# Attention and a feed-forward on one core: scores on quarters of the array, four sums on VectorE, q's turn ahead of the queue, a product between two steps

## The chip, the cores and the metric

The kernel runs on one core of a Trainium2 chip. The metric is the device time of one execution in microseconds (us). The kernel before took 1366.23 us (median of three runs, 1366.04 to 1366.33).

The core's engines have queues of their own and run beside each other. In this text PE is TensorE (matrix products, into the eight banks of PSUM), DVE is VectorE, ACT is ScalarE, POOL is GpSimd, and SP is SyncE, which here only issues DMAs. Each engine takes its instructions in the order in which the code issues them.

## The reference

The first part is attention with normalized q and k: batch 8, 12 heads, 448 tokens, head size 64.

```python
def rmsnorm(x, g):
    rms = np.sqrt(np.mean(x * x, axis=-1, keepdims=True) + 1e-06)
    return x / rms * g
q_n, k_n = (rmsnorm(q, g_q), rmsnorm(k, g_k))
scores = (1.0 / np.sqrt(64)) * np.matmul(q_n, k_n.transpose(0, 1, 3, 2))
attn = softmax(scores)
attn_out = np.matmul(attn, v)
```

Its output is laid out as `x` with 3584 tokens (8 x 448) and 768 columns (12 x 64). The second part is a feed-forward with 2048 inner columns:

```python
h = np.maximum(x @ w_in, 0.0)
return (h * h @ w_out).astype(np.float32)
```

`w_in` (768 x 2048) and `w_out` (2048 x 768) arrive as 64-bit floats; everything else is float32.

## The kernel before

**Pairs of heads.** Attention works on 48 pairs: pair `i` holds two heads (index `e`) of one batch, so that their 2 x 64 columns fill 128 partitions. Its q and k are turned into `qT` and `kT` of 128 x 448. Keys come in blocks `m` of 128: three whole ones (`NJ = 3`) and a rest of 64, and the rests of an even pair and the next odd one are worked on together (`m == NJ`). `score` multiplies block `m` of keys with all queries, for both heads, into two banks; ACT's exponential (`weigh`, line 468) reads them and takes k's norm as its scale. POOL adds the weights up (`add_up`, L487), `attend` (L552, L567, L588) multiplies them with v, and the sums over keys (L604, L622, L631) divide at the end.

`score` has two forms. Where `whole(i)` holds (pairs 25 and on), a block of keys is cut in halves of 64: four matmuls with 64 rows and 64 columns, each on a quarter of the array (L449). Elsewhere it is two matmuls with 64 rows and 128 columns (L460). The rests are always in quarters (L460). A float32 matmul is two instructions in the profile, and a weight load stands before each.

**Turning q and k.** Early pairs are turned by PE (`turn`, L415, and L418 for the rest) after POOL has scaled q (L219). Pairs from 14 on are turned by DVE in blocks (`turn_blocks`, L372), from a layout that DMAs have brought; for q, ACT then multiplies with the gains (L382). `turn_among` puts this into the queue `tasks`, whose entries (squares, row sums, divisions, turns) are issued one or two for each product of the feed-forward.

**Feed-forward in units.** Unit `u` takes the four half batches of batches `2u` and `2u + 1` with two halves of the columns as a 2 x 2 block matrix, and makes each product by seven half-size products instead of eight, with sums of blocks on both sides. The inner columns come in four blocks; each has a first product (into `hid`, followed by relu and square on ACT) and a second one with `w_out` (L1216 for the rows that are left over, L1274). Unit 0 runs beside the attention of pairs 13 to 24, units 1 and 2 beside the later ones, and the last unit, 3, alone. In units 1 to 3 the first product uses the seven-product form twice, one inside the other (`deep_products`, L1077).

**Weights.** Pieces of the weights are loaded, converted to float32 (ACT L1698 to L1701, DVE L1712 and L1731) and summed into the forms that the seven products need. These sums wait in `sums_to_make` and are issued by `make_sum` (L1807), one for each step of the stream; `sum_engines` hands them to DVE and POOL in turn. For a `w_out` tile they are T1, T3, T2, T4, in this order; T2 is made from T1 and T4 from T2. In the second product of unit 0, P5 uses T1, then P6 uses T2 and P4 uses T4. The four sums of the left side are POOL's (L1202). Two `w_out` tiles belong to a block; the first block's weights are ready during the first stage, the others' in the block before their use or in their own.

**The last unit.** Its first products run in 28 steps of 11 matmuls, cut into four parts each and interleaved: part 2 and 3 of a step stand between parts of the next. After part 2 and part 3, DVE and ACT add the banks into `whole_hid`; each block ends with joins on POOL and DVE (L1134). The second products are in two levels as well and run in rounds (`ROUNDS`, L1602): for each form of `w_out`, named `right`, the inner forms are its quarters and their sums. `sum_right` makes these (L744): for the first round (`n = 0`) its sums 0, 1 and 2 on POOL during the first products, and sum 3 on DVE at the start of the round. `multiply_rest` (L1510) makes the products of 128 rows that no round covers, in four calls: at the first round and at `right == "21"` the two parts of the left half, at `"22"` and behind the last round the two parts of the right half.

Of the kernel before, what the change touches and what calls it, by code (L numbers as in the profile page):

```python
# [23 lines left out]
P = 128  # L24
# [201 lines left out]
def program(ctx, tc, rows, v, g, wide, ones, moe_w_in, moe_w_out, out, shift):  # L226
# [216 lines left out]
    def score(i, m):  # L443

        scs = banks_of(i, m)
        if whole(i) and m < NJ:
            for e, sc in enumerate(scs):
                for half in range(2):
                    nc.tensor.matmul(  # L449
                        sc[ds(half * D, D)],  # L450
                        lhsT=turned[i, 1][ds(e * D, D), ds(m * P + half * D, D)],
                        rhs=turned[i, 0][ds(e * D, D), :], start=True, stop=True,
                    )
            return
# [922 lines left out]
    def last_unit():  # L1377
# [46 lines left out]
        def sum_right(n, m):  # L1424
            b11, b12, b21, b22 = [right_of(n, t, k) for t in range(2) for k in range(2)]
            t1, t2, t4 = [more_rights[n % 2][:, k] for k in range(3)]
            dst, left, right = ((t1, b12, b11), (t2, b22, t1), (t4, t2, b21), (b12, b22, b12))[m]
            less(nc.vector if m == 3 else nc.gpsimd, dst, left, right)()

        for n, cost in enumerate(  # L1430
# [3 lines left out]
            if n == 28:  # L1434
                load_right(0)
                load_rest("11")
            elif n in (60, 64, 68, 72):
                sum_right(0, (n - 60) // 4) if n < 72 else None
        ffn_p.release()
# [9 lines left out]
        bank_sets = [[banks[n] for n in (0, 2, 3)], list(roles)]  # L1449
        rest_banks = [banks[4], banks[1]]  # L1450

# [49 lines left out]

        def multiply_rest(a, half, n):
            ends = n == len(ROUNDS) - 1
            size = Q if ends else HALF
            for at in range(0, HALF, size):
                some = slice(at, at + size)
                for blk in range(NBLK):
                    for t in range(2):
                        last = blk == NBLK - 1 and t
                        nc.tensor.matmul(  # L1510
                            rest_banks[half][:, some], lhsT=flat[a][:, blk, t, ds(NT * P, P)],
                            rhs=rights[n % 2][:, 2 * blk + t, some],
                            start=blk + t == 0 and n in (0, 4),
                            stop=bool(last and n not in (0, 4)), skip_group_check=True,
                        )
                if n not in (0, 4):
                    to = rest_acc[:, half * HALF + at : half * HALF + at + size]
                    nc.scalar.copy(to, rest_banks[half][:, some])
                    nc.sync.dma_start(
                        out[ds(2 * u * S + P * NT, P), ds(half * HALF + at, size)], to  # L1520
                    )

        def store_pair(pair, acc, e, half):
# [37 lines left out]
        for n, (name, right) in enumerate(ROUNDS):  # L1561
            if right == "11":
                multiply_rest(0, 0, n)
            elif right == "21":
# [170 lines left out]
    def make_weight_forms(kind, dst, t):  # L1735
# [7 lines left out]
        (in_sb if kind == "in" else out_sb)[t] = dst  # L1743
        sums_to_make.extend(todo)
        if kind == "out":
# [55 lines left out]
    def make_sum():  # L1801
# [3 lines left out]
        if sums_to_make:  # L1805
            to, left, right, op = sums_to_make.popleft()
            next(sum_engines).tensor_tensor(out=to, in0=left, in1=right, op=op)  # L1807
        elif forms_to_store:
            later.append([3, partial(nc.sync.dma_start, *forms_to_store.popleft())])
# [309 lines left out]
    def turn_among(i, x):  # L2119
        if in_blocks(i):  # L2120
            tasks.append(lambda: turn_blocks(i, x))
        else:
# [84 lines left out]
```

## Time and profile before

| | before |
|---|---|
| median of three runs | 1366.23 us |
| the profiled execution | 1367.66 us |
| its span, first to last instruction | 1365.9 us |
| PE busy | 1337.1 us (98%) |
| DVE / ACT / POOL busy | 874.6 / 612.5 / 769.6 us |
| attention alone | 0 to 128 us |
| first unit beside attention | 128 to 476 us |
| last unit's first products | 1094 to 1210.5 us |
| last unit's rounds | 1210.5 to 1365.9 us |

The profile is of one execution. A row of the timeline gives the start and length in us, engine, line, operation, output and inputs, shape, and the number of instructions merged; in brackets the idle time of the engine before it and what ended that. For PE, `64*128` is rows times columns of the array in use. A row of groups gives, behind the count, the busy us and the mean ns of one, then the idle time before them.

### The profile page before, as it was taken

The page shows a single profiled execution, that of the slowest core. Times are in us where ns is not written, and L with a number is a line of the kernel's source. Part 1 is how long each engine was busy: PE and PEld are TensorE (multiplying, and loading weights), DVE is VectorE, ACT ScalarE, POOL GpSimd, SP SyncE. Part 2 cuts the span into 40 slices and gives each one's busy share as a digit, 9 for nine tenths or more (in the row PEclk, how much of TensorE's full clock was granted, in tenths as well). Part 3 has the DMA queues.
Part 4 walks back from the last instruction along what each step waited for, and adds up shares of the span by engine and source line. Part 5 has one row for each costly group of instructions (what it writes and reads, how often), then busy time and mean ns, then how long its engine had stood idle before and what let it go on. Part 6 is the DMA issues. An engine that isn't in the chain of part 4 may idle for free.

```text
span 1365.9 us, 20475 instructions
## 1 busy us (share of the span) xinstructions
PE 1337.1 (98%) x6672; PEld 887.9 (65%) x6672; DVE 874.6 (64%) x1728; ACT 612.5 (45%) x1135; POOL 769.6 (56%) x751
## 2 busy tenths in 40 slices
PE   7999999999999999999999999999999999999998
PEld 3333444444444477676858577675858599999997
DVE  4897555886768766555556866556555855456672
ACT  6985576757757144343434344343433134330000
POOL 5668754655565879577567879577555732110010
PEclk9999999999999999999999999999999999999999
DMA  5666846967849877584847767674736465544542
GB/s 136 164 182 158 211 104 158 273 186 190 270 117 284 256 193 224 142 224 107 253 104 214 216 174 226 162 216 123 237 82 227 143 194 192 155 138 150 156 161 90
DMA packets 416632, 245.61 MB, mean 180 GB/s; under 512 B 273284, under 2 KB 381060, under 8 KB 415492
## 3 DMA queue, kind: packets, MB, share of 16 engines
q1 hardware_dynamic: 416224, 244.15, 63.3%
q8 instruction: 55, 0.90, 0.3%
q14 instruction: 61, 0.50, 0.1%
q10 hardware_dynamic: 292, 0.07, 0.0%
HBM read 178.13 MB, written 65.99 MB: 179 GB/s over the span
## 4 chain that ended last, share of the span: by engine, by line
PE 82%; DVE 5%; DMA 3%; POOL 3%; ACT 2%; issue 2%; SPq 2%; POOLq 0%; ACTq 0%; DVEq 0%
PE bank L1077 25%; PE bank L1274 19%; PE bank L1602 9%; PE bank L1016 7%; PE bank L449 4%; PE bank L567 4%; PE bank L460 4%; PE bank L552 3%; PE bank L1510 2%; PE bank L588 1%; PE bank L604 1%; DVE acc L1638 1%; DMA in_sb<-in_deep 1%; PE bank L631 1%; PE bank L1216 1%
## 5 line engine op out<-in xcount | busy, mean ns | idle before, releaser
L1077 PE MATMUL bank<-xT,in_sb 128*128 128x224 f32 x1344 | 287.0, 353 | 0.0
L1077 PEld LDWEIGHTS bank<-xT,in_sb 128*128 128x128 f32 x1344 | 253.1, 190 | 9.4 <-ACT wT L468 5.6
L468 ACT ACTIVATE wT<-bank,rr 128x448 f32<-128x448 f32 x288 | 163.9, 631 | 159.4 <-PE bank L449 98.1
L1274 PE MATMUL bank<-out_sb,hid 128*128 128x384 f32 x576 | 205.9, 490 | 2.8 <-POOL out_sb L1807 1.4
L204 POOL TENSOR_TENSOR rr<-ms,minus_half 128x8 f32<-128x8 f32 (+1 forms) x96 | 145.7, 1517 | 69.2 <-DVE ms L197 58.9
L1638 DVE TENSOR_TENSOR acc<-acc,bank 128x384 f32<-128x384 f32 x231 | 122.1, 546 | 77.1 <-PE bank L1274 59.1
L1274 PEld LDWEIGHTS bank<-out_sb,hid 128*128 128x128 f32 x576 | 107.7, 190 | 82.3 <-issue 7.7
L1274 PE MATMUL bank<-out_sb,sums 128*128 128x384 f32 x432 | 156.0, 491 | 1.3 <-DVE acc L1638 0.9
L1016 PE MATMUL bank<-xT,in_sb 128*128 128x448 f32 x336 | 131.8, 546 | 0.0
L1274 PEld LDWEIGHTS bank<-out_sb,sums 128*128 128x128 f32 x432 | 80.3, 190 | 67.2 <-issue 4.8
L487 POOL TENSOR_TENSOR sum<-sum,wT 128x448 f32<-128x448 f32 (+1 forms) x96 | 112.9, 1197 | 7.5 <-ACT wT L468 6.0
L1016 PEld LDWEIGHTS bank<-xT,in_sb 128*128 128x128 f32 x336 | 62.1, 190 | 68.8 <-issue 61.7
L460 PE MATMUL bank<-qT,kT 64*128 64x448 f32 (+1 forms) x492 | 102.7, 571 | 3.4 <-ACT qT L382 2.3
L1060 DVE TENSOR_TENSOR hid<-hid,bank 128x224 f32<-128x224 f32 x208 | 73.4, 382 | 43.9 <-PE bank L1077 40.8
L487 POOL TENSOR_TENSOR sum<-wT 128x448 f32<-128x448 f32 x48 | 55.8, 1184 | 66.4 <-ACT wT L468 66.4
L449 PE MATMUL bank<-qT,kT 64*64 64x448 f32 x552 | 76.1, 540 | 0.7 <-ACT wT L468 0.7
L460 PEld LDWEIGHTS bank<-qT,kT 64*128 64x128 f32 (+1 forms) x492 | 35.4, 166 | 63.5 <-issue 35.8
L1077 PE MATMUL bank<-more,in_sb 128*128 128x224 f32 x288 | 74.4, 353 | 0.8 <-DVE whole_hid L1060 0.8
L567 PE MATMUL bank<-wT,vt 64*64 64x448 f32 x576 | 73.9, 545 | 0.0
L382 ACT ACTIVATE qT<-qT,g 128x448 f32<-128x448 f32 x34 | 22.7, 666 | 111.1 <-DVE qT L372 111.1
L1701 ACT ACTIVATE words<-words 128x384 f16<-128x384 f32 x64 | 68.5, 1071 | 2.0
L1549 POOL TENSOR_TENSOR acc<-acc 128x768 f32<-128x768 f32 x2 | 4.3, 2136 | 106.3 <-DVE acc L1500 99.4
(200 smaller groups left out, 2401.9 us busy)
## 6 DMA issues: line engine op xcount, KB each, us to landing
in_sb<-in_deep SPq DMA_DIRECT2D x64, 384.0 KB, 3.8
in_sb<-in_deep SPq DMA_DIRECT2D x80, 256.0 KB, 4.4
out_sb<-out_forms SPq DMA_DIRECT2D x48, 384.0 KB, 5.6
words<-in_moe_w_in_dram SPq DMA_DIRECT2D x32, 384.0 KB, 3.7
words<-in_moe_w_out_dram SPq DMA_DIRECT2D x32, 384.0 KB, 3.6
out_forms<-out_sb SPq DMA_DIRECT2D x8, 1536.0 KB, 6.4
qk<-in_q_dram SPq DMA_DIRECT2D x96, 96.0 KB, 2.5
qk<-in_k_dram SPq DMA_DIRECT2D x96, 96.0 KB, 2.6
```

The lines of the kernel that those rows point to most:

```text
L204: self.nc.gpsimd.tensor_tensor(out=self.rr[i][:, x, 0 : self.count(i)], in0=ms, in1=self.minus_half.to_broadcast(list(ms.shape)), op=ALU.pow,)
L449: nc.tensor.matmul(sc[ds(half * D, D)], lhsT=turned[i, 1][ds(e * D, D), ds(m * P + half * D, D)], rhs=turned[i, 0][ds(e * D, D), :], start ...
L460: nc.tensor.matmul(sc[some], lhsT=turned[p, 1][r, keys], rhs=turned[p, 0][r, :], start=True, stop=True,)
L468: nc.scalar.activation(new_weights((i, m), e), sc, AF.Exp, scale=rows.rr[i][:, 1, 2 * m + e : 2 * m + e + 1],)
L487: nc.gpsimd.tensor_tensor(out=sums[i, e][some], in0=left[some], in1=weights[key_of(i, m), e][some], op=ALU.add)
L567: nc.tensor.matmul(bank[ds(e * D, D), :], lhsT=values[i][keys, n, e, :], rhs=weights[(i, n), e][keys], start=n == 0, stop=n == NJ - 1 and ...
L1016: nc.tensor.matmul(ps, lhsT=w_sb[:, IN.index(left), c, :], rhs=forms[u, c][right], start=first and c == 0, stop=c == NK - 1, skip_group_ch ...
L1060: nc.vector.tensor_tensor(out=quarter(blk, name, n), in0=quarter(blk, base, n), in1=ps, op=ALU.add)
L1077: nc.tensor.matmul(ps, lhsT=left, rhs=right, start=start, stop=stop, skip_group_check=True)
L1274: nc.tensor.matmul(ps, lhsT=lefts[left][:, t, ts(tt, P)], rhs=w_sb[t][:, OUT.index(right), :], start=first and t == 0, stop=t == 1, skip_g ...
L1602: nc.tensor.matmul(ps, lhsT=left[l][:, blk], rhs=rest_of[r][:, blk], start=blk == 0 and product in ("P1", "P5", "P4"), stop=blk == NBLK - ...
L1638: nc.vector.tensor_tensor(out=acc, in0=acc, in1=ps, op=ALU.add)
```

## The change

Six edits:

- `score` cuts the three whole blocks of keys into quarters for all pairs.
- `sum_right` always uses DVE, and the three sums for the first round come at n = 66, 70 and 74 of the last unit's first products instead of 60, 64 and 68.
- `multiply_rest` is moved up in the last unit. The first call is divided: the products of three of the four blocks are issued at n = 110, between the last step's part 2 and its part 3, those of the fourth block where all of them were.
- The two parts of `multiply_rest` for the right half use quarters of the columns, in two banks, where the last call had them in one bank and the third a whole half.
- The fourth sum (T4) of each `w_out` tile goes to DVE; the others take turns as before.
- `turn_among` puts q's turn at the head of `tasks`, k's at the end as before.

```diff
     def score(i, m):
 
         scs = banks_of(i, m)
-        if whole(i) and m < NJ:
+        if m < NJ:
             for e, sc in enumerate(scs):
                 for half in range(2):
...
-            less(nc.vector if m == 3 else nc.gpsimd, dst, left, right)()
+            less(nc.vector, dst, left, right)()
+
+        rest_banks = [banks[4], banks[1]]
+
+        def multiply_rest(a, half, n, blks=range(NBLK)):
+            size = Q if half else HALF
+            for x, at in enumerate(range(0, HALF, size)):
+                ps = rest_banks[half - x][:, 0:size]
+                for blk in blks:
+                    for t in range(2):
+                        nc.tensor.matmul(
+                            ps, lhsT=flat[a][:, blk, t, ds(NT * P, P)],
+                            rhs=rights[n % 2][:, 2 * blk + t, at : at + size],
+                            start=blk + t == 0 and a == half, stop=blk == NBLK - 1 and t == 1 and a != half,
+                        )
+                if a != half:
+                    some = ds(half * HALF + at, size)
+                    nc.scalar.copy(rest_acc[:, some], ps)
+                    nc.sync.dma_start(out[ds(2 * u * S + P * NT, P), some], rest_acc[:, some])
...
             if n == 28:
                 load_right(0)
                 load_rest("11")
-            elif n in (60, 64, 68, 72):
-                sum_right(0, (n - 60) // 4) if n < 72 else None
+            elif n in (66, 70, 74):
+                sum_right(0, (n - 66) // 4)
+            elif n == 4 * 7 * NBLK - 2:
+                multiply_rest(0, 0, 0, range(NBLK - 1))
...
             if right == "11":
-                multiply_rest(0, 0, n)
+                multiply_rest(0, 0, n, range(NBLK - 1, NBLK))
...
-        sums_to_make.extend(todo)
+        for n, some in enumerate(todo):
+            sums_to_make.append((*some, nc.vector if kind == "out" and n == 3 else None))
...
-            to, left, right, op = sums_to_make.popleft()
-            next(sum_engines).tensor_tensor(out=to, in0=left, in1=right, op=op)
+            to, left, right, op, engine = sums_to_make.popleft()
+            (engine or next(sum_engines)).tensor_tensor(out=to, in0=left, in1=right, op=op)
...
         if in_blocks(i):
-            tasks.append(lambda: turn_blocks(i, x))
+            (tasks.append if x else tasks.appendleft)(lambda: turn_blocks(i, x))
```

The old `multiply_rest`, with its bank list, is taken out:

```diff
-        def multiply_rest(a, half, n):
-            ends = n == len(ROUNDS) - 1
-            size = Q if ends else HALF
-            for at in range(0, HALF, size):
-                some = slice(at, at + size)
...
-                            rest_banks[half][:, some], lhsT=flat[a][:, blk, t, ds(NT * P, P)],
```

More of the change, by code (lines that the diff above doesn't have):

```diff
@@ L1449, in last_unit @@
         bank_sets = [[banks[n] for n in (0, 2, 3)], list(roles)]
-        rest_banks = [banks[4], banks[1]]
         def tokens(name, pair, some):
@@ L1500, in put @@
                 nc.vector.tensor_tensor(out=dst, in0=base, in1=ps, op=op)
-        def multiply_rest(a, half, n):
-            ends = n == len(ROUNDS) - 1
-            size = Q if ends else HALF
-            for at in range(0, HALF, size):
-                some = slice(at, at + size)
[L1507 to L1510, printed above, removed]
-                            rest_banks[half][:, some], lhsT=flat[a][:, blk, t, ds(NT * P, P)],
[L1512 to L1521, printed above, removed]
         def store_pair(pair, acc, e, half):
```

## The prediction

> **What bounds the kernel now.** I read the page first (span, engines, chain of waits), then the busy time by stage.
>
> ```profile
> span 1365.9 us, 20475 instructions
> PE 1337.1 (98%) x6672; PEld 887.9 (65%) x6672; DVE 874.6 (64%) x1728; ACT 612.5 (45%) x1135; POOL 769.6 (56%) x751
> PE 82%; DVE 5%; DMA 3%; POOL 3%; ACT 2%; issue 2%; SPq 2%; POOLq 0%; ACTq 0%; DVEq 0%
> ```
> ```profile
> 0.00:128.00 128.00, 116.19 (x714) 45.48 (x715) 97.57 (x231) 99.70 (x182) 81.70 (x77) 1.00 0.63 165
> 128.00:476.00 348.00, 343.50 (x1143) 157.45 (x1142) 239.00 (x423) 217.57 (x379) 216.21 (x183) 1.00 0.75 202
> ```
>
> In the second fence the columns behind each stage's length are PE, weight loads, DVE, ACT and POOL. PE is the bound nearly everywhere, at the full clock, and carries 82% of the chain. Time can come only from PE's own work or from its few stalls. In the first stage (attention alone) ACT is busy for 99.7 us of 128 and DVE for 97.6, so PE has close followers there; in the second (first unit of the feed-forward) PE stands for 4.5 us of 348.
>
> I make the sum against the profiled execution, 1367.66 us around a span of 1365.9; the three timed runs had a median of 1366.23, 1.43 less, and I carry the difference over.
>
> **(a) Scores on quarters.** Only the 25 pairs up to number 24 change; later ones have quarters already. One pair's products on PE, and quarters where the kernel has them:
>
> ```profile
> 60.20 1.02 PE L460 MATMUL bank<-qT,kT 64*128 64x448 f32 x4
> 61.15 0.98 PE L588 MATMUL bank<-wT,lasts 64*64 64x448 f32 x8
> 62.06 0.57 PE L604 MATMUL bank<-part,ones 128*32 128x448 f32 x2
> 63.70 1.77 PE L460 MATMUL bank<-qT,kT 64*128 64x448 f32 x8
> 65.41 0.55 PE L415 MATMUL bank<-wide,qk 128*128 128x128 f32 x3
> ...
> 484.67 0.93 PE L449 MATMUL bank<-qT,kT 64*64 64x448 f32 x8
> 485.42 0.93 PE L567 MATMUL bank<-wT,vt 64*64 64x448 f32 x8
> ```
>
> Start to start, a block of keys in two 64x128 tiles takes 0.95 us (60.20 to 61.15), a set of four quarters by itself 0.91 (61.15 to 62.06), and one directly behind other quarters 0.75 (484.67 to 485.42): the array is not emptied between equal shapes. So the first two blocks of keys, now 1.71 (63.70 to 65.41), take 0.91 + 0.75 = 1.66: 0.05 gained. The third block and the quarters next to it (L588, or the joint rests of L460), now 0.95 + 0.91, take 1.66 too: 0.20 gained. That is 0.25 us a pair: 13 pairs before 128 us, 12 after.
>
> Weight loads double in number, but the 0.75 us hold four quarters' loads as well, so I add nothing. [...]
>
> How much of it reaches the end? After 128 us PE is the bound, but for the stretch before 353 us and the last one before 476 (both under b and c): nine of the twelve pairs, 2.2 us, of which I take **2.0**. Before 128 us the bounds are 0 (ACT's queue sets the pace) and 3.2 (13 pairs). With ACT and DVE so close behind I take **0.9**, nearer to the lower.
>
> **(b) q ahead of queued work.** Two of the twelve turns are late now:
>
> ```profile
> 172.55 1.92 PE L460 MATMUL bank<-qT,kT 64*128 64x448 f32 x8
> 174.65 0.65 ACT L382 ACTIVATE qT<-qT,g 128x448 f32<-128x448 f32 x1
> 175.36 0.97 PE L460 MATMUL bank<-qT,kT 64*64 64x448 f32 x4 [0.88 <-ACT qT L382]
> 176.26 0.91 PE L1216 MATMUL bank<-out_sb,hid 128*128 128x384 f32 x2
> ...
> 352.85 0.65 ACT L382 ACTIVATE qT<-qT,g 128x448 f32<-128x448 f32 x1
> 353.55 0.97 PE L460 MATMUL bank<-qT,kT 64*64 64x448 f32 x4 [1.44 <-ACT qT L382]
> ```
>
> The joint rests need the next pair's q; the scaled q comes late, and their two halves run one after the other. From 172.55 to 176.26 are 3.71 us against 0.95 + 0.91: 1.85 lost. At 353.55 the marked idle time is 0.56 longer: 2.40 lost. Put first among the tasks, the turn is issued one or two products of the stream earlier; it makes SP issue at once what is still queued of its load, and what it overtakes (the next pair's squares and row sums, the division) comes one place later. In these two no DMA is marked as late. At 175 what it overtakes (the last activations of hid, L1185/L1186) is needed only by the last quarter of L1216, some 4 us on. **1.85**.
>
> At 353 the next wait is near: POOL's queue of weight sums, which starts from ACT's last activation of hid and not from PE, and the q scaling (0.65) now stands ahead of that. With it goes
>
> **(c) one weight sum of four on VectorE.** T4 of each w_out tile goes to DVE without taking a turn of the alternation. Six turns are left for two tiles, so the second tile's turns swap: T1 and T2 go to POOL, T3 and T4 to DVE. In the second w_out tile's sums in the first unit's second block:
>
> ```profile
> 263.65 5.43 PE L1216 MATMUL bank<-out_sb,hid 128*128 128x384 f32 x16
> 264.06 1.41 POOL L1202 TENSOR_TENSOR sums<-hid 128x384 f32<-128x384 f32 x1 [4.54 <-ACT hid L1186]
> 271.10 1.12 POOL L1807 TENSOR_TENSOR out_sb<-out_sb 128x384 f32<-128x384 f32 x1
> 271.49 2.74 PE L1274 MATMUL bank<-out_sb,sums 128*128 128x384 f32 x8
> 271.74 0.90 DVE L1807 TENSOR_TENSOR out_sb<-out_sb 128x384 f32<-128x384 f32 x1
> 272.30 2.75 POOL L487 TENSOR_TENSOR sum<-sum,wT 64x448 f32<-64x448 f32 x2
> 275.12 1.01 POOL L1807 TENSOR_TENSOR out_sb<-out_sb 128x384 f32<-128x384 f32 x1
> 276.18 0.91 PE L1274 MATMUL bank<-out_sb,hid 128*128 128x384 f32 x2 [0.71 <-POOL out_sb L1807]
> ...
> 353.02 1.13 POOL L1202 TENSOR_TENSOR sums<-hid 128x384 f32<-128x384 f32 x1 [3.01 <-ACT hid L1186]
> ```
>
> Today PE waits at 276.18 for T4 from POOL. In the code's order T2 stands between the two adds of L487 at 272.30, so on POOL it ends near 274.6; DVE reaches T4 then and needs up to 0.9, as at 271.74. But PE's S2·T2 wants it three products of 0.64 after 271.49, at 273.4: a wait of 1.2 there, and T4 is ready when PE comes for it, at about 275.95 instead of 276.18. Gain **0.2**, and **0.2** for the fourth block, where the same pattern stands. In the third, L1216 follows the rests of 353.55 by 0.9, at 354.45; by (b) it would start some 2.1 us earlier, near 352.35. T2 ends 10.5 after POOL's start (264.06 to 274.6), which is 353.02 and with the q scaling ahead 353.6: 364.1. PE's need, 9.75 after the start of L1216 (263.65 to 273.4), is 362.1. So it waits 2.0 of the 2.4; bounds 0 and 2.4, I take **0.4**.
>
> In the first block, during attention alone, the swap looks bad:
>
> ```profile
> 115.31 0.67 DVE L423 TENSOR_SCALAR qT<-bank,g 128x448 f32<-128x448 f32 x1
> 116.35 1.00 POOL L1807 TENSOR_TENSOR out_sb<-out_sb 128x384 f32<-128x384 f32 x1
> ```
>
> T2 takes POOL's place of 116.35 and ends at 117.35. T4 stands behind it on DVE, then the scaled q of L423 and the next row sums, on which POOL's scaling and PE's transposes wait. T4 ends near 118.0 where q began at 115.31: DVE is 2.7 late, part of it beside PE's other work. Between +0.3 and -2.7 I take **-0.7**, and **0.2** for the first tile, whose T4 no longer stands in POOL's queue.
>
> **(d) The first form's inner sums.** Three POOL sums beside DVE's joins, and what DVE needs for one alone:
>
> ```profile
> 1151.89 1.82 POOL L744 TENSOR_TENSOR more_right<-right,more_right 128x768 f32<-128x768 f32 x1
> 1152.87 3.47 DVE L1134 TENSOR_TENSOR whole_hid<-whole_hid,part 128x448 f32<-128x448 f32 x2
> 1156.99 0.65 PE L1077 MATMUL bank<-words,in_sb 128*128 128x224 f32 x2 [1.05 <-DVE whole_hid L1060]
> ...
> L744 DVE TENSOR_TENSOR right<-right 128x768 f32<-128x768 f32 x3 | 2.9, 958 | 7.8 <-DMA more_right<-second_forms 4.0 <-PE bank L1510 3.4 <-issue 0.5
> ```
>
> Two joins take 3.47 us here and 1.15 where POOL is idle (1211.23, below); PE then waits 1.05. [...]
>
> On DVE the three cost 0.96 each, 4.16 us apart, behind evictions; the gaps there are about 0.5, so at most 3 x (0.96 - 0.5) is lost. The banks have a product's time in hand. Bounds -0.35 (1.05 less 1.4) and +1.05: **1.0**.
>
> **(e) Rests between the last steps.**
>
> ```profile
> 1209.86 0.65 PE L1077 MATMUL bank<-more,in_sb 128*128 128x224 f32 x2 [0.78 <-DVE whole_hid L1060]
> 1210.72 5.32 PE L1510 MATMUL bank<-right,whole_hid 128*128 128x384 f32 x16
> 1211.23 1.15 DVE L1134 TENSOR_TENSOR whole_hid<-whole_hid,part 128x448 f32<-128x448 f32 x2
> 1212.30 0.69 DVE L1491 TENSOR_TENSOR qk<-whole_hid 128x512 f32<-128x512 f32 x1
> 1215.88 1.46 PE L1602 MATMUL bank<-right,whole_hid 128*128 128x192 f32 x8
> ```
>
> Before the last step PE waits 0.78 for an add. Twelve of the sixteen L1510 instructions (3.9 us) go into that hole; the last step then runs at 1213.0, four follow, and the first round starts 0.85 earlier. Cover is lost: DVE still has the add, two joins (1.15) and S1 (0.69), ready at about 1215.9; PE wants it one product (1.3) after 1215.0, so it just fits. **0.85**, and -0.5 if it does not.
>
> **(f) The last halves in two banks.**
>
> ```profile
> 1356.78 2.87 PE L1510 MATMUL bank<-right,whole_hid 128*128 128x192 f32 x16 [0.41 <-ACT acc L1518]
> ```
>
> The wait for ACT's copy goes, with the emptied pipeline behind it: **0.55**, at the very end. The round with two quarters streams the same columns.
>
> **The sum.** 2.0 + 0.9 + 1.85 + 0.2 + 0.2 + 0.4 - 0.7 + 0.2 + 1.0 + 0.85 + 0.55 = 7.45. 1367.66 - 7.45 = 1360.2 profiled; timed **1358.8**.
>
> **Rivals.** *Slower:* T4 holds DVE. DVE is in order, so if POOL reaches T2 late, the evictions behind T4 stand and PE's banks stay full. T3 ran at 271.10, 7 us after POOL's first sum was ready at 264.06. Were T2 that far behind DVE in all four blocks, less the 1.3 of two products in the banks, 4 x 5.7 = 23 us would be lost: 1381.6; slower begins at (7.45 + 2.7)/4 = 2.5 us a block. Against it: POOL reaches T2 at 273.5, DVE T4 at 274.5. *Only the end gains:* scores and T sums are swallowed by ACT, DVE and POOL before 476 us; what is left is 1.85 + 2.4 = 4.25: 1362.0. For it the 99.7 us of ACT. *Quarters bring nothing* in mixed company: 2.9 less, 1361.7. *Everything is PE:* the 3.2 of (a), 2.4 at 353, no loss in the first block: 2.3 + 2.0 + 0.7 more, 1353.8.
>
> **How the numbers follow.** Forecast 0.58, only the end 0.18, quarters for nothing 0.05, everything 0.14, slower 0.05. The range 1355.0 to 1362.5 holds the forecast, most of the two weak gains and part of the strong one. A measurement tells 0.2%, 2.7 us, from no change: faster means under 1363.5. That is all but the slower case and a weak gain that fails at the end as well: 0.90 faster, 0.06 same, 0.04 slower.
>
> **What would show it.** L460 with 64*128 gone, and pairs 0.25 us shorter between 205 and 260; no wait for ACT's q at 175 and 353; a new wait for POOL's out_sb at S2·T2; joins of 0.6 us each near 1150; PE without waits at 1209 and 1356. I am wrong if DVE stands long before L1807 or the first stage keeps its length and loses more at its end.

## The result

The changed kernel took 1359.28 us (median of 6 runs, 1358.35 to 1359.76) against 1366.17 for the kernel before beside it: a ratio of 0.9946, 95% interval 0.9934 to 0.9959, or 6.9 us. A second measurement of the same kernel (below) gave 0.9959 (0.9946 to 0.9973).

The page of the changed kernel and its busy time in two stages (columns as in the prediction: length, PE, weight loads, DVE, ACT, POOL, clock, DMA share, GB/s):

```profile
span 1357.8 us, 21104 instructions
PE 1329.6 (98%) x6988; PEld 884.7 (65%) x6988; DVE 873.9 (64%) x1735; ACT 610.3 (45%) x1135; POOL 761.3 (56%) x744
PE 85%; POOL 4%; DVE 3%; issue 3%; DMA 2%; ACT 2%; SPq 1%; POOLq 0%; ACTq 0%; DVEq 0%
```
```profile
0.00:128.00 128.00, 114.17 (x871) 43.24 (x872) 96.02 (x233) 99.87 (x183) 81.54 (x77) 1.00 0.63 165
128.00:476.00 348.00, 342.19 (x1299) 156.71 (x1299) 242.75 (x432) 215.70 (x380) 217.13 (x183) 1.00 0.76 206
```

PE is busy 7.5 us less and still 98% of the span. Stages cut at fixed times don't show where, because work slides through the cuts. So the working view is another: one and the same PE instruction looked up in both timelines. Its start before minus its start after is all that the change has gained up to there. In the last column, "T sums" are waits for the weight sums T1 to T4, or for evictions that stand beside them; an eviction is DVE's adding of a finished bank to `acc` (L1636; L1638 before).

| instruction of PE | before | after | gained so far | what lies between |
|---|---|---|---|---|
| L415, first pairs | 15.21 | 14.68 | 0.53 | start, before the change acts much |
| L588 of the rests | 115.48 | 113.62 | 1.87 | quarters: +1.3 |
| L415, next pair | 120.37 | 120.24 | 0.13 | T4 in the first block: -1.7 |
| L1016 of w_in | 155.12 | 154.46 | 0.67 | quarters: +0.5 |
| L1016, the next but one | 156.00 | 156.46 | -0.46 | a wait for hid: -1.1 |
| L1216 | 176.26 | 174.63 | 1.62 | q in time: +2.0 |
| L552 | 232.26 | 230.36 | 1.91 | quarters: +0.3 |
| L1016 | 235.73 | 232.92 | 2.82 | q in time, not foreseen: +0.9 |
| L1216, second block | 263.65 | 260.59 | 3.06 | quarters: +0.2 |
| L552 behind its L1274 | 278.20 | 275.17 | 3.03 | the T sums: 0.0 |
| L1216, third block | 354.45 | 348.83 | 5.62 | quarters +0.35, q in time +2.2 |
| L552 behind its L1274 | 367.44 | 364.39 | 3.05 | the T sums: -2.6 |
| L1016 | 413.93 | 409.69 | 4.24 | quarters +0.3, q in time, not foreseen: +0.9 |
| L1216, fourth block | 441.85 | 437.37 | 4.48 | quarters: +0.2 |
| L552 behind its L1274 | 455.92 | 452.41 | 3.51 | the T sums: -1.0 |
| L1274 | 476.68 | 472.57 | 4.11 | a wait of before missing, by chance: +0.6 |
| L1077 | 1149.34 | 1145.35 | 3.99 | nothing in 670 us |
| first round | 1215.88 | 1209.88 | 6.01 | inner sums +1.0, rests +1.0 |
| last rounds | 1353.44 | 1347.47 | 5.97 | nothing |
| end of the span | 1365.86 | 1357.85 | 8.01 | last halves +0.7; the rest mostly chance, below |

Two executions of the same code differ in this view as well. The run with the last unit's edits alone (below) changes nothing ahead of 1149 us; by the same instructions it is 0.4 us ahead of before at 50 us, 0.9 at 476 (0.5 of it comes between 456 and 476, where the table has its +0.6) and 1.6 at 1149. So a single row of a few tenths shows little; the rows of 1 us and more have instructions below.

**The rows behind it.** At 175 the two halves of the joint rests (eight L460) run side by side, without a wait; before, L1216 came 3.71 us after the third block of keys, here 1.66:

```profile
172.97 0.98 PE L449 MATMUL bank<-qT,kT 64*64 64x448 f32 x8
173.77 0.93 PE L460 MATMUL bank<-qT,kT 64*64 64x448 f32 x8
174.63 1.56 PE L1216 MATMUL bank<-out_sb,hid 128*128 128x384 f32 x4
```

At 353 they nearly do: q's scaling ends at 347.89, so one half starts some 0.3 us late, and L1216 comes at 348.83:

```profile
347.62 1.28 PE L460 MATMUL bank<-qT,kT 64*64 64x448 f32 x8
```

In the first block T4 stands on DVE for 3.10 us behind POOL, with q (L423) behind it; PE waits for q, POOL for the row sums, and PE then for POOL:

```profile
114.39 1.02 POOL L1806 TENSOR_TENSOR out_sb<-out_sb 128x384 f32<-128x384 f32 x1
115.44 1.17 DVE L1806 TENSOR_TENSOR out_sb<-out_sb 128x384 f32<-128x384 f32 x1 [3.10 <-POOL out_sb L1806]
116.53 0.67 DVE L423 TENSOR_SCALAR qT<-bank,g 128x448 f32<-128x448 f32 x1
117.35 1.74 PE L449 MATMUL bank<-qT,kT 64*64 64x448 f32 x16 [1.16 <-DVE qT L423]
117.95 1.32 POOL L204 TENSOR_TENSOR rr<-ms,minus_half 128x6 f32<-128x6 f32 x1 [1.75 <-DVE ms L197]
120.24 0.55 PE L415 MATMUL bank<-wide,qk 128*128 128x128 f32 x3 [1.16 <-POOL qk L219]
```

In the third and the fourth block PE waits at the product of the sums S2 and T2 (S2·T2, L1274 on sums), for an eviction and for T2:

```profile
359.06 0.91 PE L1274 MATMUL bank<-out_sb,sums 128*128 128x384 f32 x2 [0.92 <-DVE acc L1636]
360.85 0.91 PE L1274 MATMUL bank<-out_sb,sums 128*128 128x384 f32 x2 [0.88 <-POOL out_sb L1806]
...
449.48 0.91 PE L1274 MATMUL bank<-out_sb,sums 128*128 128x384 f32 x2 [1.96 <-POOL out_sb L1806]
```

Before, there was no wait in the third block, and in the fourth 0.24 for an eviction and then this one, for T4:

```profile
454.28 0.91 PE L1274 MATMUL bank<-out_sb,hid 128*128 128x384 f32 x2 [0.69 <-POOL out_sb L1807]
```

And the last unit: joins of 0.58 each (L1134), the rests between the last steps, all last halves in one run of 32:

```profile
1148.88 1.16 DVE L1134 TENSOR_TENSOR whole_hid<-whole_hid,part 128x448 f32<-128x448 f32 x2
...
1203.96 4.03 PE L1438 MATMUL bank<-right,whole_hid 128*128 128x384 f32 x12
1207.83 0.54 PE L1077 MATMUL bank<-more,in_sb 128*128 128x224 f32 x2
1209.88 1.30 PE L1600 MATMUL bank<-right,whole_hid 128*128 128x192 f32 x7
...
1347.63 5.36 PE L1438 MATMUL bank<-right,whole_hid 128*128 128x192 f32 x32
1353.04 0.32 ACT L1445 COPY acc<-bank 128x192 f32<-128x192 f32 x1 [2.28 <-PE bank L1438]
```

From the last copy to the end of the span are 4.5 us here (1353.36 to 1357.85). Before:

```profile
1359.68 0.32 ACT L1518 COPY acc<-bank 128x192 f32<-128x192 f32 x1 [2.96 <-PE bank L1510]
```

That is 5.9 us (1360.00 to 1365.86). In the four profiles with the old end it is 4.5 to 6.1 (4.5 with T4's edit alone, 6.1 with q's alone), in the ten with the new one 4.3 to 5.4 (5.4 with the end's edits alone). So most of the 1.4 can be chance; whether the new end shortens this stretch a little stays open. Without the 1.4, 6.6 is left of the 8.0 us between the two profiled executions (1367.66 and 1359.64), near the timed 6.9.

### The profile page after: what moved, and what is told of

It is laid out like the page before. It is cut to its first block, busy times and chain, and to the rows that moved or that the text cites. A ratio compares the mean times of both kernels' runs of the same rounds, so it can differ in the third digit from the quotient of the medians.

```text
span 1357.8 us, 21104 instructions
## 1 busy us (share of the span) xinstructions
PE 1329.6 (98%) x6988; PEld 884.7 (65%) x6988; DVE 873.9 (64%) x1735; ACT 610.3 (45%) x1135; POOL 761.3 (56%) x744
## 4 chain that ended last, share of the span: by engine, by line
PE 85%; POOL 4%; DVE 3%; issue 3%; DMA 2%; ACT 2%; SPq 1%; POOLq 0%; ACTq 0%; DVEq 0%
PE bank L1077 26%; PE bank L1274 21%; PE bank L1600 9%; PE bank L1016 8%; PE bank L449 7%; PE bank L567 4%; PE bank L552 3%; PE bank L1438 2%; PE bank L460 1%; PE bank L588 1%; PE bank L631 1%; PE bank L1216 1%; PE bank L622 1%; POOL rr L204 1%; DMA words<-in_moe_w_in_dram 1%
## 5 line engine op out<-in xcount | busy, mean ns | idle before, releaser
L1077 PE MATMUL bank<-xT,in_sb 128*128 128x224 f32 x1344 | 287.0, 353 | 0.0
L1077 PEld LDWEIGHTS bank<-xT,in_sb 128*128 128x128 f32 x1344 | 253.2, 190 | 9.4 <-ACT wT L468 5.6
L1274 PE MATMUL bank<-out_sb,hid 128*128 128x384 f32 x576 | 205.7, 489 | 0.5 <-DMA out_sb<-out_forms 0.5
L1636 DVE TENSOR_TENSOR acc<-acc,bank 128x384 f32<-128x384 f32 x231 | 122.2, 546 | 74.8 <-PE bank L1274 55.1
L1274 PE MATMUL bank<-out_sb,sums 128*128 128x384 f32 x432 | 157.4, 493 | 5.9 <-POOL out_sb L1806 2.8
L1274 PEld LDWEIGHTS bank<-out_sb,hid 128*128 128x128 f32 x576 | 107.9, 190 | 79.6 <-issue 6.7
L449 PE MATMUL bank<-qT,kT 64*64 64x448 f32 x1152 | 146.6, 552 | 3.1 <-DVE qT L423 2.3
L1016 PE MATMUL bank<-xT,in_sb 128*128 128x448 f32 x336 | 131.9, 546 | 1.0 <-DVE hid L1179 1.0
L1274 PEld LDWEIGHTS bank<-out_sb,sums 128*128 128x128 f32 x432 | 79.8, 190 | 73.8 <-DVE acc L1636 9.2
L1016 PEld LDWEIGHTS bank<-xT,in_sb 128*128 128x128 f32 x336 | 62.1, 190 | 70.5 <-issue 60.8
L449 PEld LDWEIGHTS bank<-qT,kT 64*64 64x64 f32 x1152 | 49.7, 133 | 77.4 <-issue 53.4
L1077 PE MATMUL bank<-more,in_sb 128*128 128x224 f32 x288 | 74.5, 354 | 0.0
L1060 DVE TENSOR_TENSOR whole_hid<-whole_hid,bank 128x224 f32<-128x224 f32 x104 | 37.7, 386 | 39.5 <-PE bank L1077 37.6
```

The costliest lines, as they stand in the source:

```text
L449: nc.tensor.matmul(sc[ds(half * D, D)], lhsT=turned[i, 1][ds(e * D, D), ds(m * P + half * D, D)], rhs=turned[i, 0][ds(e * D, D), :], start ...
L1016: nc.tensor.matmul(ps, lhsT=w_sb[:, IN.index(left), c, :], rhs=forms[u, c][right], start=first and c == 0, stop=c == NK - 1, skip_group_ch ...
L1060: nc.vector.tensor_tensor(out=quarter(blk, name, n), in0=quarter(blk, base, n), in1=ps, op=ALU.add)
L1077: nc.tensor.matmul(ps, lhsT=left, rhs=right, start=start, stop=stop, skip_group_check=True)
L1274: nc.tensor.matmul(ps, lhsT=lefts[left][:, t, ts(tt, P)], rhs=w_sb[t][:, OUT.index(right), :], start=first and t == 0, stop=t == 1, skip_g ...
L1636: nc.vector.tensor_tensor(out=acc, in0=acc, in1=ps, op=ALU.add)
```

## The experiments

**One part at a time, in the kernel before.** Quarters:

```diff
-        if whole(i) and m < NJ:
+        if m < NJ:
```

> Only the scores on quarters, in the kernel before. As I predicted: 0.25 us a pair, 0.9 before 128 us and 2.0 after it, so 2.9 us less than before, about 1363.3 us. Rival (ACT, DVE and POOL swallow it): under 0.7 us, about 1365.5. What the trace of the changed kernel suggests: 1.35 of gain by 115 us; whether it lives on past 155 us, where the changed kernel has a wait of 1.15 us for hid, is open: if the wait at 155 belongs to any kernel that comes there early, it stands in this run too.

Measured: 1366.75 against 1366.78, ratio 0.9999 (0.9990 to 1.0008): nothing. The gain is made and then lost twice. By 150 us PE is 1.7 us ahead; then it waits 1.3 at 155.13 for hid, as the changed kernel does. At 353 it comes early for a q that comes no earlier, and after that wait the granted clock falls to a half for 3.41 us. PE, and the busy time in that stretch and in the one ahead of it (columns as above):

```profile
352.95 0.97 PE L460 MATMUL bank<-qT,kT 64*64 64x448 f32 x4 [2.13 <-ACT qT L382]
353.85 7.12 PE L1216 MATMUL bank<-out_sb,hid 128*128 128x384 f32 x16
```
```profile
351.00:354.42 3.42, 1.47 (x6) 0.63 (x7) 3.35 (x8) 3.32 (x7) 1.93 (x2) 1.00 1.00 347
354.42:357.83 3.41, 3.41 (x7) 1.73 (x6) 0.68 (x1) 2.69 (x5) 3.33 (x4) 0.50 1.03 300
```

The sixteen L1216 take 7.12 us instead of 5.43 (the prediction's row at 263.65). Of the timed executions, five had a mean clock of 0.997 or 0.998 and took 1367.06 to 1368.13; six had 0.999 or 1.000 and took 1365.44 to 1366.75. The medians of the two groups, 1367.38 and 1365.68, lie 1.7 us apart, about what one such fall costs.

q's turn:

```diff
-            tasks.append(lambda: turn_blocks(i, x))
+            (tasks.append if x else tasks.appendleft)(lambda: turn_blocks(i, x))
```

> Only q's turn ahead of queued work, in the kernel before. As I predicted: the two late turns at 175 and 353 us go, 1.85 us at 175 and between 0 and 2.4 at 353, so 1362.0 to 1364.3. New theory: there are four late turns, since in the kernel before the second half of the joint rests starts at 234.83, right when ACT's q (234.11 for 0.67) ends, and the other half ran by itself ahead of it, so that no idle time was marked; the same near 412. Then 0.75 us more at each, 1360.5 to 1362.8, and the stretches at 232 and 413 us of before get shorter by 0.7 to 0.9 each in this run and not in that of the quarters.

Measured: 1363.43, ratio 0.9976 (0.9967 to 0.9985): 3.35 us, the four late turns rather than two. The kernel before had one near 234, with no idle time marked: ACT's scaled q (234.11 to 234.78) comes in the middle of the three sets of L460, the last of which has to wait for it; the twelve take 2.65 us.

```profile
233.16 2.65 PE L460 MATMUL bank<-qT,kT 64*128 64x448 f32 x12
...
234.11 0.67 ACT L382 ACTIVATE qT<-qT,g 128x448 f32<-128x448 f32 x1 [1.41 <-DVE qT L372]
```

With q ahead, the same twelve take 1.94:

```profile
231.65 1.94 PE L460 MATMUL bank<-qT,kT 64*128 64x448 f32 x12
233.52 1.77 PE L1016 MATMUL bank<-xT,in_sb 128*128 128x448 f32 x4
```

By the same instructions in both timelines the run gains 1.8 at 175, 0.7 here, 2.0 at 353 and 0.7 at 412. But the 2.0 of 353 are gone by 367, in waits for an eviction (0.89 at 361.66) and for POOL's T4 (0.58 at 363.15), with T4 where it always was.

T4 on VectorE:

```diff
-        sums_to_make.extend(todo)
+        for n, some in enumerate(todo):
+            sums_to_make.append((*some, nc.vector if kind == "out" and n == 3 else None))
...
-            to, left, right, op = sums_to_make.popleft()
-            next(sum_engines).tensor_tensor(out=to, in0=left, in1=right, op=op)
+            to, left, right, op, engine = sums_to_make.popleft()
+            (engine or next(sum_engines)).tensor_tensor(out=to, in0=left, in1=right, op=op)
```

> Only T4 on VectorE, in the kernel before. As I predicted: +0.2 in the first tile, -0.7 in the first block, +0.2 each in the second and fourth, nothing in the third (q is late there anyway): about 1366.3, no change. New theory, from the changed kernel's trace: the first block loses 1.8, the others 0 to 1.1 each, as VectorE's evictions and the sum T2 come late: 1368 to 1370. Rival: the loss near 117 us in the changed kernel comes from its being 1.9 us early there, and here it is under 0.5 us.

Measured: 1368.33, ratio 1.0012 (1.0003 to 1.0021): 1.55 us slower. The rival falls: PE is only 0.7 us ahead of before here at 115, against 1.9 in the changed kernel, and loses 2.3 in the first block:

```profile
117.20 1.16 DVE L1808 TENSOR_TENSOR out_sb<-out_sb 128x384 f32<-128x384 f32 x1 [3.09 <-POOL out_sb L1808]
...
119.10 1.77 PE L460 MATMUL bank<-qT,kT 64*128 64x448 f32 x8 [1.67 <-DVE qT L423]
```

The last unit's edits, without the quarters, q's turn and T4:

```diff
-            less(nc.vector if m == 3 else nc.gpsimd, dst, left, right)()
+            less(nc.vector, dst, left, right)()
...
+            elif n == 4 * 7 * NBLK - 2:
+                multiply_rest(0, 0, 0, range(NBLK - 1))
...
+                ps = rest_banks[half - x][:, 0:size]
```

> Only the edits of the last unit (inner sums on VectorE, rests between the last steps, last halves in two banks), in the kernel before. As I predicted: 1.0 + 0.85 + 0.55 = 2.4, so 1363.8. From the changed kernel's trace: 0.97 + 1.05 + 0.68 = 2.7, so 1363.5. Rival: the stretch from the last copy to the end, 5.9 us in before's profiled execution and 4.4 in the changed kernel's, is shortened by the edit as well: 4.1 less, 1362.1; if it is only what one execution differs from another, it is between 4.4 and 5.9 in these four profiles whatever their edits.

Measured: 1363.28, ratio 0.9978 (0.9969 to 0.9987): 3.5 us, an interval that holds 2.4 as well as 2.7. In the profile the edits gain 0.97, 1.0 and 0.7. The stretch behind the last copy is 5.4 us, 0.5 under before's and 0.9 over the one of T4's run, whose end has no edit: the rival's 1.4 us are not seen, but a smaller gain there is not excluded.

The four parts alone make 0.0 + 3.35 - 1.55 + 3.5 = 5.3 us, the change 6.9. The difference is not much beyond what the intervals leave open, but one cause has a row: quarters have no late q to run into once q is ahead.

**The changed kernel with one part taken back.** Quarters off:

```diff
-        if m < NJ:
+        if whole(i) and m < NJ:
```

> The changed kernel with the scores of the first pairs back on 64x128 tiles. As I predicted (quarters are worth 2.9): 1362.3. Theory: alone they are worth nothing, because what they gain before 155 us is lost at the stores, and what they gain before 353 at the late q; with q in time the second part lives: 1.3 to 2.0, so 1360.7 to 1361.4, a ratio of 0.9956 to 0.9963. Rival: nothing in any company, 1359.4.

Measured: 1362.29, ratio 0.9968 (0.9956 to 0.9980), and the changed kernel beside it 1360.80, 0.9959 (0.9946 to 0.9973). So quarters are worth 1.5 us in this company, by intervals that overlap; by the same instructions in two profiles they are worth 2.6 up to 490 us. (The run without them falls back by another 1.9 us between 490 and 1149, where both run the same code.)

T4 back in the alternation:

```diff
-        for n, some in enumerate(todo):
-            sums_to_make.append((*some, nc.vector if kind == "out" and n == 3 else None))
+        sums_to_make.extend(todo)
...
-            to, left, right, op, engine = sums_to_make.popleft()
-            (engine or next(sum_engines)).tensor_tensor(out=to, in0=left, in1=right, op=op)
+            to, left, right, op = sums_to_make.popleft()
+            next(sum_engines).tensor_tensor(out=to, in0=left, in1=right, op=op)
```

> The changed kernel with T4 back in the alternation of VectorE and GpSimd; the other edits stay. Theory (T4 on VectorE costs what the runs so far show, less what other waits swallow): 0.9 us in the first block, where 1.8 are lost at 117 us but a wait at 155 us for DMA stores would take half back; 0.3 in the third and 0.95 in the fourth block. So some 2 us faster than the changed kernel, a ratio to before near 0.9930 where the changed kernel has 0.9946, about 1357.3. Rival (by my prediction T4's move is worth 0.3 us): no change against the changed kernel, 1359.5.

Measured: 1359.38, ratio 0.9948 (0.9934 to 0.9961): no change, against my theory, though the interval would hide one of 1 us. In its profile PE is 1.1 us ahead of the changed kernel at 441 us and 0.5 behind at 454: two waits close together, and the clock falls to a half again, for 3.41 us from 449.76. PE, then the stretches:

```profile
448.00 0.91 PE L1274 MATMUL bank<-out_sb,hid 128*128 128x384 f32 x2 [1.14 <-DVE acc L1636]
449.60 1.53 PE L1274 MATMUL bank<-out_sb,hid 128*128 128x384 f32 x2 [0.68 <-POOL out_sb L1805]
451.05 2.75 PE L552 MATMUL bank<-wT,vt 128*64 128x448 f32 x8
```
```profile
448.00:450.00 2.00, 1.32 (x3) 0.68 (x4) 0.00 (x0) 0.00 (x0) 1.92 (x3) 0.94 1.18 303
450.00:454.00 4.00, 4.00 (x14) 0.98 (x16) 2.21 (x5) 0.00 (x0) 2.95 (x4) 0.60 1.10 311
```

Whether the timed executions fell into it as often isn't known.

T4 on VectorE, but using up its turn, so that T1, T2 and T4 of every tile are VectorE's and no order is swapped:

```diff
-            (engine or next(sum_engines)).tensor_tensor(out=to, in0=left, in1=right, op=op)
+            turn_of = next(sum_engines)
+            (engine or turn_of).tensor_tensor(out=to, in0=left, in1=right, op=op)
```

> The changed kernel, with T4 on VectorE but taking its turn of the alternation: T1, T2 and T4 of every tile on VectorE, T3 on GpSimd, so that T4 no longer waits for GpSimd. Theory (the harm is the swap of turns, which puts T2 on GpSimd and T4 behind it): no wait for GpSimd's out_sb at 361 and 449 us, the first block loses under 0.5 at 117, 1.5 to 2.5 us faster than the changed kernel, 1357 to 1358. Rival (the harm is VectorE's time: each sum takes 0.9 to 1.3 there, ahead of evictions): the waits for VectorE's acc at 271 and 359 stay or grow to 1.5 or more, and the time is 1359 or more.

Measured: 1357.63, ratio 0.9936 (0.9922 to 0.9950). No wait for GpSimd's out_sb is left, nor the one for q at 117, and PE gains 1.4 us on the changed kernel between 115 and 125; the waits for acc stay, with 0.9 to 1.0 of marked idle time each. The swap is the larger harm, as far as intervals that overlap the changed kernel's can tell.

**The wait at 155 us.** Each block of w_in is kept in DRAM in two kinds of forms: raw ones, in five stores straight from `in_sb` (L1756, L1758), and derived ones, which are sums of those (L1766) with stores of their own. In the changed kernel DVE has to have a free buffer for a derived form and stands 7.49 us for the store of an earlier one; PE waits behind it:

```profile
152.60 0.69 DVE L1766 TENSOR_TENSOR more<-in_sb 128x512 f32<-128x512 f32 x1 [7.49 <-DMA in_deep<-more]
...
155.98 2.52 PE L1016 MATMUL bank<-xT,in_sb 128*128 128x448 f32 x6 [0.98 <-DVE hid L1179]
```
```profile
144.00:148.00 4.00, 4.00 (x23) 1.76 (x23) 1.12 (x2) 2.63 (x5) 3.90 (x4) 1.00 1.04 287
148.00:152.00 4.00, 4.00 (x12) 2.07 (x11) 0.00 (x0) 0.64 (x2) 2.39 (x3) 1.00 0.97 256
```

The DMA engines are full there (shares of 1.04 and 0.97, the column before the last). In the kernel before, DVE stood there as well:

```profile
152.15 0.69 DVE L1767 TENSOR_TENSOR more<-in_sb 128x512 f32<-128x512 f32 x1 [7.10 <-DMA in_deep<-more]
```

DVE goes on at nearly the same time, 152.15 and 152.60; PE, which was not held up then, now comes earlier and has to wait. The edit: the five raw stores behind the derived ones, in all blocks, once with T4's edit and once without.

```diff
-        return [raw] + [lambda make=make: both(make) for make in steps + [None, None]]
+        return [lambda make=make: both(make) for make in steps + [None, None]] + [raw]
```

> The changed kernel with one edit: the five raw stores of a block's w_in forms are issued behind the stores of its derived forms, not ahead of them. Theory: the wait of 1.15 us at 155.98 is VectorE held for a free buffer of the derived forms (7.49 us idle), because their stores stand behind the raw ones while the DMA engines are full from 144 us on; then it goes, and about 1.1 us with it: 1358.3. Rival (the DMA engines are full whatever the order): the wait moves or stays, no change, 1359.4.

> The changed kernel without T4 on VectorE, and with the raw stores last. Theory: both gains and the part of the first that the wait at 155 us swallows: 2.0 + 1.1 + 0.9 = 4.0 less than the changed kernel, 1355.4. Rival (raw stores do not matter): as without T4 alone, about 1357.3.

Measured: 1380.26, ratio 1.0094 (1.0079 to 1.0109), and 1376.84, 1.0079 (1.0065 to 1.0093). The wait at 155 goes, as the theory says (1.25 gained at 161 us), and each of the three later blocks pays some 6 to 8 us: in_sb is not free for the next weights until the raw stores have read it, and DVE stands with the evictions behind it. PE waits 5.1 to 7.5 us in each, and there the clock falls to a half for 6.8 to 10.2 us; the mean clock of all nine executions is 0.990 to 0.993.

```profile
270.35 0.36 DVE L1710 TENSOR_SCALAR in_sb<-words 128x384 uint32<-128x384 uint32 x1 [11.56 <-DMA in_deep<-in_sb]
...
272.78 2.93 PE L1274 MATMUL bank<-out_sb,hid 128*128 128x384 f32 x4 [6.98 <-DVE acc L1636]
```

So only the first block, where nothing presses on in_sb, and T4 with its turn kept:

```diff
-        return [raw] + [lambda make=make: both(make) for make in steps + [None, None]]
+        steps = [lambda make=make: both(make) for make in steps + [None, None]]
+        return [raw] + steps if blk else steps + [raw]
```

> The changed kernel with T4 on VectorE taking its turn, and in the first block of the first unit alone the raw stores of w_in behind those of the derived forms. Theory: the wait at 155 us is VectorE's, for a buffer whose store stands behind the raw ones; it goes, with nothing late behind it, since the inputs of the first block are not overwritten soon: 1.1 to 1.3 us less than with the turn kept, about 1356.3, a ratio of 0.9922 to 0.9932. Rival: the raw stores are missed somewhere else, as in the kernel with all of them last (7 us waits at 273, 370 and 474): 1362 or more.

> The changed kernel itself, unedited, beside the next two. A ratio to before near 0.9946 again. In its profile the stretch from the last copy to the end lies between 4.4 and 6.1 us, as in the other profiles. Open: whether the wait of 2.1 us at 449 us is followed by some 3.4 us at half the granted clock, as the waits of 2.3 us at 353 in the kernel with quarters alone and of 1.3 + 0.8 us at 449 in the one without T4 were; the first profile of the changed kernel shows none.

Measured: 1354.70, ratio 0.9920 (0.9906 to 0.9933); the changed kernel beside it 1360.80, 0.9959 (0.9946 to 0.9973). The intervals do not touch: 6.1 us faster than the changed kernel, 11.6 faster than before. In the profile 1.4 of it comes between 115 and 120 us, by the turn kept, and 1.25 at 155, by the stores; by the timed runs the stores' part is not told apart from nothing, since the intervals with and without them (0.9922 to 0.9950) overlap. PE runs through 155 in one group, and near 449 one wait is left:

```profile
149.64 6.55 PE L1016 MATMUL bank<-xT,in_sb 128*128 128x448 f32 x17
...
444.88 1.86 PE L1274 MATMUL bank<-out_sb,hid 128*128 128x384 f32 x4 [0.74 <-DVE acc L1636]
```

The second profile of the changed kernel has its wait at 449 again (1.94 us), again without a fall of the clock, and 4.5 us behind the last copy.

The same without T4's edit:

> The changed kernel with T4 back in the plain alternation and the first block's raw stores last: against the fastest kernel so far (ratio 0.9920) it differs in T4 alone. Theory (T4 on VectorE with its turn kept pays by itself, since PE's two waits near 449 us, 1.3 and 0.85, become one of 0.9 to 1.2 and no half clock follows): 0.6 us more at 361 us, 0.9 at 449 and up to 1.7 where the half clock follows, a ratio of 0.9930 to 0.9943. Rival (the gain of that kernel is the stores' alone): 0.9920.

Measured: 1358.13, ratio 0.9937 (0.9923 to 0.9950). The median is 3.4 us above the one with T4 on VectorE and its turn kept, but the intervals overlap, and the two profiles differ by 0.4 us ahead of the end; no half clock shows. That T4 pays by itself there stays open.

## Why the prediction was right, and where it was not

The time and its size came out (1359.28 against 1358.8); several terms did not, and their errors cancelled. Both signs of being wrong that the prediction names came, in the first block: DVE stood 3.10 us before its sum at 115.44, and of the 1.87 us gained by 115 all but 0.13 were lost again by 120, so that the first stage nearly kept its length.

- **(a) Quarters, 2.0 + 0.9.** The price per pair held. In two profiles of the changed kernel, with and without quarters, they are worth 2.6. Weight loads did not eat it: there are 6988 instead of 6672, and they take 884.7 us instead of 887.9. But the step that split the gain by how close ACT's queue is was not what decided. Before 128 us 1.3 to 1.9 were gained, not 0.9 (1.5 in the run alone), and then 1.1 to 1.3 went at 155, at DVE's buffers and full DMA engines, which the working does not have. Alone the part is worth nothing.
- **(b) q ahead.** 1.85 at 175: 2.0 in the changed kernel, 1.8 by itself. Right, mechanism and size. At 353 it was 2.2 of the 2.40. "Two of the twelve turns are late" was wrong: four are. I counted by marked idle time, and where two halves share the array, PE is marked busy with one while the other is missing (at 233.16, 2.65 us without a mark against 1.94 with q in time). The two that I missed are worth 0.7 each by themselves.
- **(c) T4, 0.2 + 0.2 + 0.4 - 0.7 + 0.2 = 0.3.** Wrong in sign in the kernel before, where the edit alone is 1.55 slower; in the changed kernel no difference is measured. In the first block the mechanism was as written, the size was not: 1.7 and not 0.7, as PE has no other work for the time. In the third I had 2.0 of 2.4 eaten; it was 2.6 of 2.2, in two waits (0.92 and 0.88 marked, 1.1 each from start to start), of which T2 is one. But 2.1 go there without T4's edit too, with q's turn alone and in the changed kernel without T4, for an eviction and for T4 on POOL: the wait was rightly seen, and most of it is not the edit's. The second and fourth, where I counted 0.2 each, gave 0.0 and -1.0: in the fourth PE waits 1.96 for T2 on POOL, where the working has 1.2. In the second, PE waits for an eviction that the working does not have. That T3, now DVE's and early, holds it up is not shown, for with q's turn alone, T3 and T4 where they were, PE waits nearly as long; the changed kernel, then q's turn alone:

```profile
270.93 1.56 PE L1274 MATMUL bank<-out_sb,sums 128*128 128x384 f32 x4 [1.04 <-DVE acc L1636]
...
273.17 1.56 PE L1274 MATMUL bank<-out_sb,hid 128*128 128x384 f32 x4 [0.89 <-DVE acc L1638]
```

- The slower rival, T4 holding DVE, had its place and its row right (3.10 us behind POOL at 115.44), and it is the reason that (c) loses in the first block; with 5.3 us in four blocks, T4's edit or not, the T sums stayed under its point of 2.5 us a block. A sum on DVE took 1.26 beside POOL's work (266.53) and 0.55 without it (273.11 in the run with all raw stores last); the edit alone cost 1.55.
- **(d) 1.0, (e) 0.85, (f) 0.55.** Measured 1.0, 1.0 and 0.7, in the rows shown: no wait at 1157, 1210 and 1357. Of (d), 1.3 came near 1157 and 0.35 went again before 1200, within the 1.4 that was allowed for. The cover of (e) held.
- "Only the end gains" falls by the table. "Quarters bring nothing" holds for the quarters alone; in the changed kernel the table and two profiles speak against it, while the timed intervals overlap. "Everything is PE" falls at 120, 155, 361 and 449 us.

By the table, which names the place of a wait and not its cause, forecast against measured: quarters 2.9 and 3.2, q 4.25 (with the 2.4 at 353) and 6.0, T sums -2.1 (with the 2.0 eaten in the third block) and -5.3, the wait at 155 nothing and -1.1, the last unit 2.4 and 2.7, the start, the wait of before near 469 and the rest nothing and 1.0. That is 7.45 and, from these rounded figures, 6.5. The T sums and the stores took 4.3 us more than forecast; the unseen turns of q gave back 1.75 of them, quarters and the last unit 0.3 each, and the last item 1.0, much of which is chance. That the total came out so near is luck: nothing in the working says that these errors would cancel.

## What to carry to other kernels

Count late operands by when the operand is ready against when its user could start, not by marked idle time: the array, shared by two streams, was not marked idle at 233.16 while one of them ran, for 2.65 us in place of 1.94. An alternation of engines is a schedule: to take one item out of it moves every later item to the other engine, so keep the turn and override only the engine. A gain ahead of a full queue was lost there (1.1 us at 155, with DMA shares of 1.04 and 0.97); look for the next fixed point (a store, a buffer, a late operand) before counting it, and move only the one transfer that stands in the way.

## What the runs showed of the hardware

In two profiles waits of PE cost about double their length. After a wait of 2.13 us in the run with quarters, and after two of 1.14 and 0.68 within 2.5 us in the changed kernel without T4, the granted clock was a half for 3.41 us, in which PE lost some 1.7 us more (the sixteen L1216 took 7.12 for 5.43); after 1.96 and 1.94 us at 449 in the two profiles of the changed kernel it stayed at 1.00.

The traces show what decides. In all 14, every change of the granted clock stands a whole number of 3.413 us behind the first one: in the changed kernel the clock rises at 15.35 and falls, behind the last product, at 1356.79, 393 such windows later. So each trace can be cut into its windows, and PE's idle time counted in each. Of some 5,480 windows at full clock that begin ahead of PE's last product, eight were followed by half the clock, with 1.82, 1.95, 2.24, 2.27 and four times 3.41 us of idle time; none of the others has more than 1.66. In the run with quarters the wait falls into one window (the row 351.00:354.42 above, 3.42 less 1.47). In the changed kernel the end of a window divides it, into 1.32 and 0.64:

```profile
445.43:448.84 3.41, 2.09 (x6) 0.68 (x4) 3.38 (x5) 0.00 (x0) 3.25 (x4) 1.00 1.03 391
448.84:452.26 3.42, 2.78 (x10) 1.40 (x12) 0.99 (x3) 0.00 (x0) 3.26 (x4) 1.00 1.15 311
```

So here the idle share of a window decided, with a limit between 1.66 and 1.82 us, and not the length of one wait. Ends of matmuls are modelled, so the limit is no more exact than that. Where the windows begin differs from profile to profile (the first change is at 13.58 to 17.02 us), so the same wait can cost a fall in one execution and not in the next; that fits the run with quarters, where five of eleven executions have the lower clock.

Issuing a DMA took longer behind the raw stores. SP's own rows of the changed kernel, first the five raw stores, then two loads of v:

```profile
140.02 2.51 SPq L1756 DMA_DIRECT2D in_deep<-in_sb  x3
142.57 2.83 SPq L1758 DMA_DIRECT2D in_deep<-in_sb  x2
145.50 3.67 SPq L323 DMA_DIRECT2D vt<-in_v_dram  x2
```

One issue takes 0.84 us, then 1.42, then 1.84, and the stores of the derived forms stand behind them on SP. In the kernel with the first block's raw stores last, loads of v take 0.6 us each ahead of those stores and 1.43 behind them:

```profile
139.11 1.23 SPq L323 DMA_DIRECT2D vt<-in_v_dram  x2
...
164.51 1.43 SPq L331 DMA_DIRECT2D vt<-in_v_dram  x1
```

A full share of the DMA engines does not do it by itself: in the changed kernel three stores of derived forms at 149.27 take 0.57 us each, with the share still at 0.97. What does is not shown.
